# A linear-attention block: buffers for weight sums, and places of a fold's transposes, x statistics and stores in the engines' queues

## The chip, the cores and the metric

The kernel runs on one core of a Trainium2 chip. A core has five engines that each work through a queue of their own in order: TensorE (PE, with its weight loads shown apart as PEld), VectorE (DVE), ScalarE (ACT), GpSimd (POOL) and SyncE (SP), which here only issues DMAs. An instruction waits at the head of its queue until the semaphores it needs have come; what stands behind it on the same engine waits too. The metric is the device time of one launch in microseconds (us). A profiled execution gives the span from the first to the last instruction, and PE's granted clock.

## The reference

All tensors are float32, with S = 2048 rows, D = 1024 columns, 32 heads of 32, and a hidden width of 3584.

```
qkv   = layernorm(x) @ wqkv                       # q, k, v: 32 heads of 32
pq,pk = q_h @ w_phi[h],  k_h @ w_phi[h]           # per head
phi   = concat(softmax(p), softmax(-p))           # for q and for k
o     = phi_q (phi_k^T v) / (phi_q sum(phi_k) + 1e-6)
h     = x + o @ wo
out   = h + relu(layernorm(h) @ w1) @ w2
```

## The kernel before

**Precision.** A float32 product is made of three matmuls: each operand is split into a high part and a low part (high by ACT with a rounding copy, low as the difference, on DVE or POOL), and `mm3` (L180 to L183) adds high x high, high x low and low x high.

**Items and steps.** The work of PE is a list of items. A projection item (`project`, L489) multiplies one tile of 128 rows of x with 8 weight units of 128x512, one unit to a step: so an item has 8 steps of three matmuls. The first half of the rows comes first: items 0 to 31 make k and v (four groups `s` of weights, each over 8 row tiles), items 32 to 47 make q (two groups). Then the second half of the rows, then attention, the output projection, and the two MLP products. The other engines' work is set beside these steps by hand: `do(n, k, f)` puts a call at step k of item n, `when(step, f)` the same with step = 8n + k. The calls are run in the order of the steps when the program is written, so a step sets the order within each engine's queue and not a time: an engine whose queue does not wait can be ahead of PE.

**Weight units.** `Units` (L68 to L136) loads each unit into one of six `raw` tiles (SP, L320 to L334) and splits it into one of ten `w` places: ACT at L124, then POOL or DVE at L128. A load is put into SP's queue as soon as, in program order, a raw tile has been split and the unit is "ready"; it waits there until that split has really been done. Two places are over when a group of 8 units is in use, so the first two splits of the next group come early and the other six follow one by one as PE leaves the old units. A group changes at steps 64, 128, 192, 256 (to q) and 320.

**The fold.** The feature weights `w_phi` are multiplied into the k and q weights on the chip, in eight parts p = 0 to 7. For part p, `wt_load` (L269) loads two tiles `wt`, `fold_part` (L281) makes 32 small matmuls into two `tp` and two `mm` banks and transposes them on DVE, eight instructions of 128x256 (L299), into the tile `wp` (one buffer); `fold_store` (L303) writes it to memory in two halves, and `fold_ready` (L309) lets `Units` load the units made of it. Parts 1 to 3 serve the k groups 1 to 3, parts 4 to 7 the two q groups. The `mm` banks (four) are also those of the items; an item's bank is given back by `kv_first` (DVE, L423 to L427).

**Weight sums.** The MLP uses sums and differences of blocks of w1 and w2. There are 56 of them to be made, number n at step 24 + 10 n (64 later from some point on): `t_load` (L343) loads a tile `b` of 128x4x256 (SP), four `t_sum` (L353, POOL) work in it, and `t_store` (L359, SP) writes it to memory. Their tile has two buffers, in the pool `tsp`.

**x statistics.** For the row tiles 8 to 15 the layer norm's statistics are made early, at steps from 80 + 16 (t - 8): `ln_load` (SP, L214), ten steps on `ln_stats` (DVE, L220 to L222), and three steps on `ln_power` (POOL, L229 to L231). `xin` has two buffers. The row tiles 1 to 7 are normalised and transposed between steps 4 and 52 with a table of their own.

Of the kernel before, what the change touches and what calls it, by code (L numbers as in the profile page):

```python
# [9 lines left out]
F32 = mybir.dt.float32  # L10
# [5 lines left out]
P = 128  # L16
S = 2048
D = 1024
# [5 lines left out]
NK = D // P  # L24
# [115 lines left out]
def kernel(  # L140
# [12 lines left out]
    v, act, pool, pe, sp = nc.vector, nc.scalar, nc.gpsimd, nc.tensor, nc.sync  # L153
# [9 lines left out]
    def mm_bank():  # L163
        return psum.tile([P, 512], F32, name="mm", bufs=4)

    def tp_bank():
        return psum.tile([P, 512], F32, name="tp", bufs=2)
# [20 lines left out]
    def do(n, k, f, *args):  # L188
        at[n, k].append((f, args))
# [17 lines left out]
    xin, xst, xnt = {}, {}, {}  # L207
# [52 lines left out]
    tsp = kps.enter_context(tc.tile_pool(name="tsum", bufs=1, side="right"))  # L260
    folds = ExitStack()
    fp = folds.enter_context(tc.tile_pool(name="fold", bufs=2))
# [3 lines left out]
    wt_of = {}  # L266
    folded = set()

    def wt_load(p, eng, cols=slice(0, D)):  # L269
        for i in range(2):  # L270
            j = 8 + 2 * p + i if p < 4 else 2 * (p - 4) + i
            if (p, i) not in wt_of:
                wt_of[p, i] = fp.tile([P, D], F32, name="wt", bufs=4)
            eng.dma_start(wt_of[p, i][:, cols], wqkT[j][:, cols])

    def fold_mm(p, k, ps, sides=(0, 1)):
# [4 lines left out]
    def fold_part(p):  # L281

        banks = [tp_bank(), tp_bank(), mm_bank(), mm_bank()]
        for i in range(2):
            w = wt_of[p, i].rearrange("e (k c d) -> e k c d", k=NK, c=4)
            for c in range(4):
                for h in range(4):
                    rows = slice(32 * h, 32 * (h + 1))
                    pe.matmul(banks[h][32 * c:32 * (c + 1), 256 * i:256 * (i + 1)], wphi[rows, (2 * p + i) % 8, :],
                              w[rows, :, c, :], start=True, stop=True)  # L290
        wp_of[p] = wp = fp.tile([P, NK, 256], F32, name="wp", bufs=1)
        for h, ps in enumerate(banks):

            if p < 4:
                dst = wp.rearrange("d k (i h f) -> d i h k f", i=2, h=4)[:, :, h]
            else:
                dst = wp.rearrange("d k (r i c f) -> d i c r k f", r=2, i=2, c=2)[:, :, h // 2, h % 2]
            for i in range(2):
                v.transpose(dst[:, i], ps[:, 256 * i:256 * (i + 1)].rearrange("p (k d) -> p k d", k=NK))  # L299

    wp_of = {}
# [38 lines left out]

    tsum = {}

    def t_load(w, p, j):  # L343
        cols = slice(256 * j, 256 * (j + 1))
        b = tsp.tile([P, 4, 256], F32, name="b", bufs=2)
        src = (w1 if w == 1 else w2)[2 * p:2 * p + 2, :, :, cols]
        sp.dma_start(b, src.rearrange("a b p f -> p (a b) f"))
        for r in range(2):
            for c in range(2):
                tsum[j, r, c] = b[:, 2 * c + r if w == 1 else 2 * r + c, :]  # L350
        tsum[j] = b
# [12 lines left out]
    def first_values():  # L364

        for k in range(0, NK, 2):
            if k == 4:
                ln_load(("x", 1), x_part(1))
            place = W.raws.take()
            t = place[1]  # L370
            sp.dma_start(t.rearrange("p (k f) -> p k f", k=2), wv[0, k:k + 2].rearrange("k p f -> p k f"))
            for i in range(2):
                first_raw[k + i] = t[:, 256 * i:256 * (i + 1)], place
        W.loaded = W.done = NK
# [460 lines left out]
    def item(gen, *args, keys):  # L835
        items.append((gen, args + (keys,)))
        steps.extend((k,) for k in keys)
        return len(items) - 1

    kv_n, q_n, wo_n, up_n, down_n = {}, {}, {}, {}, {}  # L840
# [9 lines left out]
    for b, tiles in enumerate(groups):  # L850
        for hf in range(2):

            pairs = b == 0 and hf == 0
            for j in range(0, 4, 2 if pairs else 1):
# [3 lines left out]
                for half in range(2):  # L858
                    n = item(wo_pair, tiles[j:j + 2], hf, half, keys=[("wo", hf, 4 * half + k // 2) for k in range(8)])
# [18 lines left out]
    def x_part(t):  # L878
        return [x[t * P:(t + 1) * P, :]]
# [6 lines left out]
    def when(step, f, *args):  # L886

        if step < 8 * first_up:
            do(step // 8, step % 8, f, *args)
        else:  # L890
            do(first_up + (step - 8 * first_up) // 4, step % 4, f, *args)
# [4 lines left out]
    for t in range(1, NT):  # L896
        n = t - 1 if t < HT else q_n[1, t - HT] + 1
        turn = 8 * n + 1
        if t < HT:
            stages = X_STEPS.get(t, (turn - 22, turn - 12, turn - 9, turn - 6, turn, turn + 3))  # L900
        else:

            early = 80 + 16 * (t - HT)
            when(early, ln_load, ("s", t), x_part(t))
            when(early + 10, ln_stats, ("s", t))
            when(early + 10, xin.pop, ("s", t))
            when(early + 13, ln_power, ("s", t))
            load_ = turn - 88 + 8 * (t - HT) if t < HT + 4 else turn - 36
            stages = (load_, None, None, turn - 8, turn, turn + 3)
        for step, f, *args in zip(stages, (ln_load, ln_stats, ln_power, ln_norm), [("x", t)] * 4):  # L910
            if step is not None:
                when(step, f, *args, *([x_part(t)] if f is ln_load else []))
        do(n, 0, x_open, t)
        for j in range(2):
            when(stages[4 + j], ln_turn, ("x", t), j, lambda t=t: xT[t])


    for i, j in enumerate((2, 3, 0, 1)):
# [1 line left out]
        if i % 2:  # L920
            when(8 * (1 + i // 2) + 2 + 4 * (i % 2) + 3, fold_store, 0, 1 - i // 2)
        when(40, fold_ready, 0, j // 2)
    for p, n in zip(range(1, 8), (3, 6, 10, 14, 18, 22, 26)):
        do(n, 6, fold_part, p)
        for j in range(2):
            when(8 * n + 6 + 5 + j, fold_store, p, j)
            when(8 * n + 6 + 13 + j, fold_ready, p, j)
        if p < 7:
            do(n - 1, 2, wt_load, p + 1, sp)


    for (hf, s, t), n in kv_n.items():
# [106 lines left out]
    def up_step(b, p, m):  # L1039

        return up0 + 4 * (up_n[b, p, m] + 1 - first_up)

    for j, m in enumerate(UP):

        for g in range(2):
            step = up0 + (8 * j + (-62, -32)[g] if j < 4 else 6 * (j - 4) + 10 + 2 * g)
# [4 lines left out]
            step = up_step(0, NP - 1, m) + 3 * j  # L1051
# [13 lines left out]
    for n, (w, p, j) in enumerate((w, p, j) for w in (1, 2) for p in range(NP) for j in range(2)):  # L1065
        step = 24 + 10 * n
        if step > 8 * q_n[1, 0] - 20:
            step += 64
        when(step, t_load, w, p, j)
        for k in range(4):  # L1070
            when(step + 7 + k, t_sum, j, k)
        when(step + 13, t_store, w, p, j)

    for b in range(2):
        for m in DOWN:
            n = down_n[b, m, NP - 1] + 1
            name, more = {1: "x1", 5: "x4", 6: "x2", 4: "x3"}.get(m), \
# [17 lines left out]
    wphi = fp.tile([P, 8, 32], F32, name="wphi", bufs=1)  # L1095
    sp.dma_start(wphi, w_phi.rearrange("(j i) e f -> i e j f", i=4))
    wt_load(0, sp, slice(0, 256))
    ln_load(("x", 0), [x[0:P, 0:512], x[0:P, 512:1024]])
    wt_load(0, sp, slice(256, D))
    first_values()  # L1100
    wt_load(1, sp)
    ident = consts.tile([P, P], F32, name="ident")
    make_identity(nc, ident)
    ones = consts.tile([P, P], F32, name="ones")
# [97 lines left out]
```

## Time and profile before

| what | value |
|---|---|
| time, median of 3 runs | 1923.57 us (1922.38 to 1924.74) |
| time of the profiled execution | 1924.54 us |
| span of the profiled execution | 1922.8 us |
| mean granted PE clock | 0.996 |
| POOL, DVE, ACT busy | 967.0, 1044.2, 741.9 us |
| DMA | 432.17 MB, 224 GB/s over the span |

A row of a timeline gives the start, the duration, the engine, the line and what it writes and reads; in brackets stands how long the engine stood idle before it and what it waited for. A row of the waits gives the engine, the line, whom it waited for, the total in us, how often, and the longest. A row of windows gives the stretch, its length, the busy time of PE, PEld, DVE, ACT and POOL, the granted clock, the DMA engines' share and GB/s. PE's rows are pipelined, so consecutive ones overlap.

### The profile page before, as it was taken

The numbers are of one execution on the slowest core, as the hardware profiler recorded it, in microseconds if no ns is written. First come the engines' busy times: TensorE is split into PE (matmuls) and PEld (weight loads), VectorE is DVE, ScalarE is ACT, GpSimd is POOL, SyncE is SP. The second block draws the span as 40 slices with busy tenths as digits, with TensorE's granted clock in tenths as the row PEclk, the third lists the DMA queues.
The fourth block names the chain that finished last, engine by engine and source line by source line (L and its number), as shares of the span: only waits on it lengthen the run. The fifth ranks groups of instructions, "written<-read, shape, count | busy, mean of one in ns | idle before, by whom it ended". The sixth has DMA issues, their size and how long they took to land.

```text
span 1922.8 us, 31955 instructions
## 1 busy us (share of the span) xinstructions
PE 1894.4 (99%) x11640; PEld 1539.5 (80%) x11640; DVE 1044.2 (54%) x1752; ACT 741.9 (39%) x1318; POOL 967.0 (50%) x935
## 2 busy tenths in 40 slices
PE   8989999999999999999999999999999999999999
PEld 7767778887877777788888888888888888888887
DVE  6867668776779866546554465333533333333333
ACT  5322225322223211245544464444444444444442
POOL 3677752789955988423333222222244444444443
PEclk9999999999999999999999999999999999999999
DMA  6877786666566657787777796656677677767775
GB/s 216 271 252 257 225 262 197 214 210 199 183 225 200 197 190 255 231 261 237 246 255 249 250 298 213 197 182 193 202 246 234 192 237 224 252 211 220 214 217 177
DMA packets 292733, 432.17 MB, mean 225 GB/s; under 512 B 24160, under 2 KB 150368, under 8 KB 292576
## 3 DMA queue, kind: packets, MB, share of 16 engines
q1 hardware_dynamic: 275680, 413.36, 67.8%
q10 hardware_dynamic: 16896, 16.78, 2.6%
q8 instruction: 91, 1.49, 0.3%
q14 instruction: 66, 0.54, 0.1%
HBM read 292.68 MB, written 137.36 MB: 224 GB/s over the span
## 4 chain that ended last, share of the span: by engine, by line
PE 83%; POOL 7%; DMA 4%; issue 2%; DVE 2%; ACT 0%; SPq 0%; POOLq 0%; DVEq 0%; ACTq 0%
PE mm L181 21%; PE mm L182 20%; PE mm L183 20%; POOL b L357 4%; PE ac L181 4%; PE ac L182 4%; PE ac L183 4%; PE tp L182 2%; PE tp L183 2%; PE tp L181 2%; POOL w L128 2%; DMA b<-in_w_dram 1%; PE tp L244 1%; DMA t<-b 1%; DMA xin<-in_x_dram 1%
## 5 line engine op out<-in xcount | busy, mean ns | idle before, releaser
L128 POOL TENSOR_TENSOR w<-raw,w 128x512 fp32r<-128x512 f32 x355 | 472.0, 1331 | 718.7 <-ACT w L124 678.0
L124 ACT ACTIVATE w<-raw 128x512 fp32r<-128x512 f32 x686 | 409.0, 626 | 516.6 <-PE mm L183 253.2
L128 DVE TENSOR_TENSOR w<-raw,w 128x512 fp32r<-128x512 f32 x331 | 269.0, 813 | 529.3 <-ACT w L124 528.6
L181 PE MATMUL mm<-w,xT 128*128 128x512 f32 x768 | 311.1, 405 | 5.0 <-DVE ke L427 5.0
L182 PE MATMUL mm<-w,xT 128*128 128x512 f32 x768 | 303.7, 395 | 12.5 <-POOL w L128 12.3
L183 PE MATMUL mm<-w,xT 128*128 128x512 f32 x768 | 301.7, 393 | 0.0
L181 PE MATMUL mm<-hT,w 128*128 128x512 f32 x672 | 262.6, 391 | 0.0
L183 PE MATMUL mm<-hT,w 128*128 128x512 f32 x672 | 261.6, 389 | 0.0
L182 PE MATMUL mm<-hT,w 128*128 128x512 f32 x672 | 261.5, 389 | 0.0
L357 POOL TENSOR_TENSOR b<-b 128x256 f32<-128x256 f32 x224 | 181.7, 811 | 108.8 <-DMA b<-in_w_dram 98.0
L182 PEld LDWEIGHTS mm<-w,xT 128*128 128x128 f32 x768 | 145.8, 190 | 47.0 <-POOL w L128 17.2
L181 PEld LDWEIGHTS mm<-w,xT 128*128 128x128 f32 x768 | 145.7, 190 | 42.5 <-issue 11.7
L183 PEld LDWEIGHTS mm<-w,xT 128*128 128x128 f32 x768 | 145.5, 190 | 30.9
L181 PE MATMUL mm<-w 128*128 128x512 f32 x392 | 152.5, 389 | 0.0
L182 PE MATMUL mm<-w 128*128 128x512 f32 x392 | 152.5, 389 | 0.0
L183 PE MATMUL mm<-w 128*128 128x512 f32 x392 | 152.5, 389 | 0.0
L183 PEld LDWEIGHTS mm<-hT,w 128*128 128x128 f32 x672 | 126.1, 188 | 26.5
L182 PEld LDWEIGHTS mm<-hT,w 128*128 128x128 f32 x672 | 126.2, 188 | 25.7
L181 PEld LDWEIGHTS mm<-hT,w 128*128 128x128 f32 x672 | 126.2, 188 | 25.7
L431 ACT ACTIVATE ke<-ke 128x512 f32<-128x512 f32 x64 | 40.4, 631 | 156.5 <-DVE ke L427 156.4
L183 PEld LDWEIGHTS mm<-w 128*128 128x128 f32 x392 | 73.6, 188 | 15.3
L181 PEld LDWEIGHTS mm<-w 128*128 128x128 f32 x392 | 73.6, 188 | 15.3
(165 smaller groups left out, 3141.7 us busy)
## 6 DMA issues: line engine op xcount, KB each, us to landing
raw<-t SPq DMA_DIRECT2D x224, 256.0 KB, 3.8
raw<-ad SPq DMA_DIRECT2D x196, 256.0 KB, 3.0
raw<-in_w_dram SPq DMA_DIRECT2D x168, 256.0 KB, 3.0
b<-in_w_dram SPq DMA_DIRECT2D x56, 512.0 KB, 4.1
t<-b SPq DMA_DIRECT2D x56, 512.0 KB, 4.5
ad<-c SPq DMA_DIRECT2D x112, 256.0 KB, 3.6
ad<-s SPq DMA_DIRECT2D x84, 256.0 KB, 3.9
ed<-qe ACTq DMA_DIRECT2D x32, 512.0 KB, 4.4
```

Of the source, the lines that this page charges most:

```text
L124: nc.scalar.activation(w[:, 0, :], raw[1], AF.Copy)
L128: eng.tensor_tensor(out=w[:, 1, :], in0=raw[1], in1=w[:, 0, :].bitcast(F32), op=ALU.subtract)
L181: pe.matmul(ps, a_hi, b_hi, start=first, stop=False, skip_group_check=more)
L182: pe.matmul(ps, a_hi, b_lo, start=False, stop=False, skip_group_check=more)
L183: pe.matmul(ps, a_lo, b_hi, start=False, stop=last, skip_group_check=more)
L244: pe.transpose(pt[:, k, :], xn[:, (4 * j + k) * P:(4 * j + k + 1) * P], ident)
L357: pool.tensor_tensor(out=tsum[j, *out], in0=tsum[j, *a], in1=tsum[j, *b], op=ALU.subtract)
L431: act.activation(e_of[key], e_of[key], AF.Exp)
```

## The change

Four things are moved, and no operation is added or left out.

- The `wt` tiles get two buffers instead of four. Part p is loaded at the beginning of item n - 2, where n is the item of its fold (part 1 at item 1 instead of in the prologue).
- The parts 2 to 7 are folded at items 8, 12, 16, 20, 24 and 28 instead of 6, 10, 14, 18, 22 and 26, part 1 one step later in item 3. `fold_part` makes only the transposes of the two `mm` banks (heads 2 and 3); those of the `tp` banks (heads 0 and 1) come four steps later, for part 1 at once. Stores come 14 and 16 steps after the fold's step instead of 5 and 6, readiness 24 and 26 steps after it instead of 13 and 14.
- The tile `b` gets two more buffers, in the fold's pool `fp`, for n with n mod 4 of 2 or 3, as long as step + 20 is before item 32, which holds for n up to 21. For all n up to 21 the sums come 12 steps behind the load instead of 7, and the store 19 instead of 13.
- The early statistics of x tiles 8 to 15 come 14 steps behind their load instead of 10, `ln_power` 17 instead of 13.

```diff
-                wt_of[p, i] = fp.tile([P, D], F32, name="wt", bufs=4)
+                wt_of[p, i] = fp.tile([P, D], F32, name="wt", bufs=2)
...
-        wp_of[p] = wp = fp.tile([P, NK, 256], F32, name="wp", bufs=1)
-        for h, ps in enumerate(banks):
-
+        wp_of[p] = fp.tile([P, NK, 256], F32, name="wp", bufs=1)
+        fold_banks[p] = banks
+        fold_turn(p, (2, 3))
+        if p == 1:
+            fold_turn(p, (0, 1))
+
+    fold_banks = {}
+
+    def fold_turn(p, heads):
+
+        wp = wp_of[p]
+        for h in heads:
+            ps = fold_banks[p][h]
             if p < 4:
...
-    def t_load(w, p, j):
+    def t_load(w, p, j, place):
         cols = slice(256 * j, 256 * (j + 1))
-        b = tsp.tile([P, 4, 256], F32, name="b", bufs=2)
+        b = place.tile([P, 4, 256], F32, name="b", bufs=2)
...
-            when(early + 10, ln_stats, ("s", t))
-            when(early + 10, xin.pop, ("s", t))
-            when(early + 13, ln_power, ("s", t))
+            when(early + 14, ln_stats, ("s", t))
+            when(early + 14, xin.pop, ("s", t))
+            when(early + 17, ln_power, ("s", t))
...
-    for p, n in zip(range(1, 8), (3, 6, 10, 14, 18, 22, 26)):
-        do(n, 6, fold_part, p)
+    for p, n in zip(range(1, 8), (3, 8, 12, 16, 20, 24, 28)):
+        do(n, 6 if p > 1 else 7, fold_part, p)
+        if p > 1:
+            when(8 * n + 10, fold_turn, p, (0, 1))
         for j in range(2):
-            when(8 * n + 6 + 5 + j, fold_store, p, j)
-            when(8 * n + 6 + 13 + j, fold_ready, p, j)
-        if p < 7:
-            do(n - 1, 2, wt_load, p + 1, sp)
+            when(8 * n + 6 + 14 + 2 * j, fold_store, p, j)
+            when(8 * n + 6 + 24 + 2 * j, fold_ready, p, j)
+        do(max(n - 2, 1), 0, wt_load, p, sp)
...
-        when(step, t_load, w, p, j)
+        far = step + 20 < 8 * q_n[0, 0]
+        when(step, t_load, w, p, j, fp if far and n % 4 > 1 else tsp)
         for k in range(4):
-            when(step + 7 + k, t_sum, j, k)
-        when(step + 13, t_store, w, p, j)
+            when(step + (12 if far else 7) + k, t_sum, j, k)
+        when(step + (19 if far else 13), t_store, w, p, j)
...
-    wt_load(1, sp)
```

## The prediction

> **What bounds the kernel now.** I read the page first, then the waits by engine for the first 310 us, then a table of windows over the same stretch, and last the timelines around each place where PE stands. A step below is one `k` of one item, as in the code: eight steps to an item, three matmuls to a step.
>
> ```profile
> PE 1894.4 (99%) x11640; PEld 1539.5 (80%) x11640; DVE 1044.2 (54%) x1752; ACT 741.9 (39%) x1318; POOL 967.0 (50%) x935
> 120.00:140.00 20.00, 14.94 (x102) 11.21 (x101) 14.46 (x33) 5.75 (x11) 13.57 (x14) 0.91 0.71 227
> 140.00:180.00 40.00, 37.64 (x344) 28.99 (x343) 25.45 (x60) 5.75 (x12) 26.04 (x36) 0.96 0.86 291
> 240.00:260.00 20.00, 16.03 (x89) 11.62 (x88) 8.79 (x14) 3.88 (x5) 16.28 (x17) 0.91 0.81 250
> 260.00:400.00 140.00, 140.00 (x764) 115.03 (x763) 108.64 (x186) 55.80 (x83) 70.91 (x75) 1.00 0.69 224
> ```
>
> PE is the bound: only standing PE time can be won, since the change takes no matmul away. In the windows' rows (length, then PE, PEld, DVE, ACT, POOL, granted clock, DMA share, GB/s) PE has holes between 120 and 260 us and none from 260 to 400. The granted clock, too, is below 1.00 in the holed stretches. These are PE's own rows after each hole, with the idle time in brackets:
>
> ```profile
> 126.70 0.39 PE L183 MATMUL mm<-w,xT 128*128 128x512 f32 x1
> 126.92 0.39 PE L181 MATMUL mm<-w,xT 128*128 128x512 f32 x1
> 132.12 0.79 PE L182 MATMUL mm<-w,xT 128*128 128x512 f32 x1 [4.81 <-POOL w L128]
> 132.71 0.63 PE L183 MATMUL mm<-w,xT 128*128 128x512 f32 x1
> 133.14 0.63 PE L181 MATMUL mm<-w,xT 128*128 128x512 f32 x1
> 135.29 0.55 PE L182 MATMUL mm<-w,xT 128*128 128x512 f32 x1 [0.25 <-POOL w L128]
> 152.47 0.75 PE L181 MATMUL mm<-w,xT 128*128 128x512 f32 x1 [2.36 <-DVE ke L427]
> 189.43 0.50 PE L182 MATMUL mm<-w,xT 128*128 128x512 f32 x1 [1.14 <-POOL w L128]
> 208.49 0.47 PE L181 MATMUL mm<-w,xT 128*128 128x512 f32 x1 [2.62 <-DVE ke L427]
> 242.76 0.50 PE L182 MATMUL mm<-w,xT 128*128 128x512 f32 x1 [1.50 <-POOL w L128]
> 245.94 0.49 PE L182 MATMUL mm<-w,xT 128*128 128x512 f32 x1 [1.51 <-POOL w L128]
> 247.85 0.63 PE L182 MATMUL mm<-w,xT 128*128 128x512 f32 x1 [0.96 <-POOL w L128]
> ```
>
> Matmuls start 126.92 - 126.70 = 0.22 us apart though one takes 0.39 (they are pipelined), so a step is about 0.67 us. The first two rows are the last before the first hole. After it they start 133.14 - 132.71 = 0.43 apart: half speed. I name the holes by their time: **A** at 132, **B** at 152, **C** at 189, **D** at 208, **E** at 243 to 248. A, C and E wait for a split of a weight on POOL (L128); B and D wait for DVE to give back a matmul bank (L427).
>
> What makes POOL and DVE late (the waits of the first 310 us: who waited at which line for whom, us in total, how often, the longest; then rows of timelines):
>
> ```profile
> POOL b L357 <- DMA b<-in_w_dram: 63.4, 16, 10.4
> DVE st L220 <- DMA xin<-in_x_dram: 29.6, 8, 8.1
> SPq L347 <- DMA t<-b: 69.0, 18, 7.6
> SPq L324 <- POOL w L128: 27.5, 9, 8.7
> 115.27 0.53 SPq L360 DMA_DIRECT2D t<-b  x1
> 122.89 0.38 SPq L347 DMA_DIRECT2D b<-in_w_dram  x1
> 127.32 0.72 POOL L357 TENSOR_TENSOR b<-b 128x256 f32<-128x256 f32 x1 [3.91 <-DMA b<-in_w_dram]
> 140.37 0.62 SPq L214 DMA_DIRECT2D xin<-in_x_dram  x1
> 146.69 1.29 DVE L220 BATCH_NORM_STATS2 st<-xin 128x6 f32<-128x512 f32 x2 [8.05 <-DMA xin<-in_x_dram]
> 175.28 1.57 POOL L357 TENSOR_TENSOR b<-b 128x256 f32<-128x256 f32 x2 [3.08 <-DMA b<-in_w_dram]
> 187.67 3.40 POOL L128 TENSOR_TENSOR w<-raw,w 128x512 fp32r<-128x512 f32 x2
> 193.42 3.46 SPq L324 DMA_DIRECT2D raw<-wpq  x2
> 202.47 1.29 DVE L220 BATCH_NORM_STATS2 st<-xin 128x6 f32<-128x512 f32 x2 [7.37 <-DMA xin<-in_x_dram]
> 227.51 2.37 POOL L357 TENSOR_TENSOR b<-b 128x256 f32<-128x256 f32 x3 [3.71 <-DMA b<-in_w_dram]
> 246.54 1.25 POOL L128 TENSOR_TENSOR w<-raw,w 128x512 fp32r<-128x512 f32 x1
> ```
>
> It is one ring. SP holds the load of `b` number n until the store of number n-2 has landed (two buffers; 69.0 us of SP's time, 18 times). POOL then stands at the sum, and behind the sum in POOL's queue stands the split that PE needs. **A**: the store went out at 115.27, the next load only at 122.89, POOL stood 3.91 us until 127.32, and only then come the sum, other work and the split; PE resumes at 132.12. **C** and **E**: POOL stands 3.08 us at 175.28 and 3.71 us at 227.51 and then works without a break into the group change; E's last split ends at 246.54 + 1.25 = 247.79, and PE resumes at 247.85. **B** and **D**: SP waits for the same late splits to free raw tiles (3.46 us at 193.42), so the load of x goes out late (140.37, and after 193.42 + 3.46 = 196.9), DVE stands 8.05 and 7.37 us at its statistics, and the bank eviction behind them is late for PE.
>
> **What the change does to these, term by term.** The number of matmuls, sums, transposes, splits and DMAs stays the same; only buffers and places in the queues move.
>
> *The holes' size.* Idle time is 4.81 + 0.25 + 2.36 + 1.14 + 2.62 + 1.50 + 1.51 + 0.96 = 15.15. The bracket starts when the last matmul has ended, 0.39 - 0.22 = 0.17 after the next one could have started: seven times 0.17 adds 1.2. Clock: 0.09 x 20 + 0.04 x 40 + 0.09 x 20 = 5.2 us lost at half speed in three places. Together **21.5 us**.
>
> Here a rule can be weighed. The trace shows half speed behind a 2.36 us hole (133 and 152 alike) and behind E's three holes, none above 1.51. The Trainium skill, page "TensorE: Matmul & The Clock Gate", section "Why this matters for your kernels", says that gaps under about 3 us keep the full clock. By it only A would cost clock, and the sum would be 18.1; the trace disagrees in B and E, and I keep 21.5.
>
> *Four buffers until the fold pool closes* (loads 0 to 21, ending at step 234). A load now waits for the store four numbers back, which is in order 21 steps before it instead of 7: 14 us against some 5. The page's landing times are these:
>
> ```profile
> b<-in_w_dram SPq DMA_DIRECT2D x56, 512.0 KB, 4.1
> t<-b SPq DMA_DIRECT2D x56, 512.0 KB, 4.5
> L357 POOL TENSOR_TENSOR b<-b 128x256 f32<-128x256 f32 x224 | 181.7, 811 | 108.8 <-DMA b<-in_w_dram 98.0
> ```
>
> A turn of a buffer is load 4.1 + four sums 3.2 (at 811 ns) + store 4.5, about 12 us. Two buffers allow one unit per 6 us, just under the 10 steps (6.7 us) that are asked; every delay stays in the ring. Four allow one per 3. With sums 12 steps (8 us) behind their load, POOL need not stand. So A goes, and C and E lose the 3 to 4 us by which POOL entered late. The store's six steps more keep SP from waiting on POOL in front of its x loads.
>
> *x statistics four steps later*: 14 steps are 9.4 us. B's x load was 146.69 - 140.37 = 6.3 us under way, D's 202.47 - 196.9 = 5.6. Issued in time they land before DVE asks; with splits no longer late SP does issue them in time. B and D go. The wait that is added is only `ln_power` on POOL, moved along by the same four steps; its consumer is the normalisation far later.
>
> *Fold later and halved.* All 7 x 8 transposes stay. In order the folds of steps 54, 86, 118, 150, 182 and 214 become 70, 102, 134, 166, 198 and 230, away from the group changes at 64, 128 and 192. The second half of the transposes lands in the gap that DVE spends on the exponent. I put no separate gain on it; below zero it could cost what it took beside a split, some 1 us for C. The two `wt` buffers: a load is now 22 steps (14.7 us) ahead of its fold's matmuls, and the buffers it takes were read 10 steps before it or earlier; the matmuls of the item beside it hide it, and PE stands if it lands later than that. I take 0.
>
> *What is late next.* (1) Item 8. Weights of the second group are loaded at step 54 instead of 43, for use at 64. SP runs ahead of PE, so the step is not the time:
>
> ```profile
> 51.70 0.22 POOL L229 TENSOR_SCALAR sc<-mv 128x1 f32<-128x1 f32 x1 [2.94 <-DVE mv L222]
> 53.52 0.42 SPq L320 DMA_DIRECT2D raw<-wpk  x1
> 74.06 0.40 PE L181 MATMUL mm<-w,xT 128*128 128x512 f32 x1
> raw<-wpk SPq DMA_DIRECT2D x56, 128.0 KB, 3.6
> L128 POOL TENSOR_TENSOR w<-raw,w 128x512 fp32r<-128x512 f32 x355 | 472.0, 1331 | 718.7 <-ACT w L124 678.0
> ```
>
> Loads went out at 53.52 for a first use at 74.06. In the new order the first sums stand behind x tile 6's power (51.70 on POOL) instead of ahead of it, the store of `b` 0 behind them, and the fold's stores and the next `b` store behind that. I estimate the raw loads at about 63: 51.7 + two rounds of sums and a zacc. The first split is ready at about 63 + 3.6 (landing) + ACT's part and POOL's, 1.3 at most each, = 69.2, under 74; but POOL then owes eight sums' rest, splits and zaccs by step 70, and the last splits come within 1 us of their use. Bounds 0 to 5 us (3 us late plus a half-speed stretch); I take **1.5**. (2) Steps 186 to 189: sums 15 now fall between the splits of the group change at 192: four sums are 3.2 us, of which some 1 us stays: **1.0**, bounds 0 to 3. (3) Step 244: load 22 has only its own pair of buffers again and follows the store of 20 by one step, not seven; POOL no longer brings along the 3.71 us that it stood at 227.51, so I take **0.5**, bounds 0 to 5. (4) Unseen rest, small waits at new places: **1.0**, bounds -1 (the prologue no longer shares its transfers with the `wt` pair that now loads at step 8) to 3.
>
> Contention between POOL and DVE is in the rows: the two splits at 187.67 took 1.70 each against 1.33 on average. The same operations overlap as before, so no term.
>
> Sum: 21.5 - 1.5 - 1.0 - 0.5 - 1.0 = **17.5 us**. The profiled execution took 1924.5 (span 1922.8 and what lies around it), 1 us above the median 1923.6; taken from the execution it gives 1907.0, from the median **1906.1**, which I predict.
>
> **The rivals.**
> *Partial.* A, B and D go, C and E stay, because POOL is short of time at a group change whatever it had before: C cost 1.14 + 0.17 = 1.3, E 3.97 + 3 x 0.17 + 1.7 of clock = 6.2, together 7.5 of the 21.5. With the new terms (1) and (3) at mid range, 2.5 each, the gain is 21.5 - 7.5 - 5 = 9: **1914.6**. For it: E's last split ends a long run of POOL work. Against it: the 3.71 us it stood just before.
> *SP stays the bound.* The raw ring, not `b`, holds SP: 27.5 us of waiting on POOL's splits (L324) remain in the code. Then x loads stay late and so do sums, and what A gives is taken at item 8: **1922**. Against it: the splits were late through `b`, as A shows.
> *Slower.* One mechanism, at item 8: SP's queue now has the fold's stores behind the store of `b` 0 and the raw loads behind the store of `b` 1. It decides from raw loads later than about 74.1 - 6.2 = 68 us; each us beyond is a us of PE, and half clock on top. If sums wait for DVE there as the row at 51.70 does, and SP stays as tight further on, holes of A's kind come back and 5 us are added: **1929**.
>
> The skill's rule of the clock, if it held for the new trace, would only lower the gain: 18.1 - 4 = 14, so 1909.5, inside the forecast's own range; it is no case by itself.
>
> **How the numbers follow.** Forecast (gain 13 to 22, 1901.5 to 1910.5) 0.57; partial (gain 4 to 13) 0.25; SP stays the bound 0.11; slower 0.07. A measurement here tells 0.2%, 3.8 us, from no change. Faster is forecast and partial, 0.82; same 0.11; slower 0.07. The range takes the forecast's upper bound with a little for terms at zero, 1900, and most of the partial case, 1918.
>
> **What would show it.** Right: in the first 310 us POOL's wait at L357 for `b` falls from 63.4 to under 15; SP's wait at L347 for `t<-b` from 69.0 to under 30; DVE's wait at L220 for x from 29.6 to under 15; no PE hole over 2 us between 100 and 230; granted clock 1.00 there; items start evenly from item 16 on. Wrong: a hole before item 9 (term 1), around step 256 (term 3), or bank waits on L427 that stay while POOL's waits are gone, which would take B and D out of my ring.

## The result and the profile after

| kernel | median us | range, runs | ratio to before, 95% interval |
|---|---|---|---|
| before | 1923.31 | 1922.38 to 1924.74, 4 | |
| changed | 1910.54 | 1908.41 to 1912.33, 4 | 0.9933 (0.9915 to 0.9950) |

The change makes the kernel 12.8 us faster, 0.67%; 17.5 had been forecast (1906.1, range 1900 to 1918). The profiled execution took 1910.06 us with a span of 1908.3. From here on, A to E are the five holes of the kernel before, at 132, 152, 189, 208 and 243 to 248 us.

Windows of the changed kernel (start and end, length, then busy PE, PEld, DVE, ACT and POOL, the granted clock, DMA share, GB/s):

```profile
70.00:90.00 20.00, 15.85 (x161) 10.95 (x160) 16.05 (x31) 7.41 (x14) 18.41 (x18) 0.91 0.53 161
120.00:140.00 20.00, 20.00 (x200) 15.43 (x201) 18.03 (x33) 6.46 (x13) 19.18 (x22) 1.00 1.02 342
140.00:180.00 40.00, 40.00 (x351) 32.32 (x344) 33.12 (x71) 10.81 (x21) 31.28 (x38) 1.00 0.98 323
220.00:240.00 20.00, 19.29 (x157) 15.20 (x156) 11.19 (x23) 7.60 (x13) 16.98 (x16) 1.00 0.74 249
```

From 120 to 180 us PE has no hole any more and runs at full clock. Of E a small one is left (0.71 us at 232). A new place stands at 70 to 90 us: 20 - 15.85 = 4.15 us without work, and clock 0.91. The waits of the first 310 us, to be read against those of before:

```profile
PE mm L182 <- POOL w L128: 4.9, 4, 3.1
POOL b L367 <- DMA b<-in_w_dram: 43.4, 11, 16.9
DVE st L220 <- DMA xin<-in_x_dram: 1.7, 1, 1.7
SPq L357 <- DMA t<-b: 25.4, 5, 7.9
SPq L334 <- POOL w L128: 15.8, 7, 5.3
```

DVE's wait for x fell from 29.6 to 1.7 us, SP's for the stores of `b` from 69.0 to 25.4, SP's for splits of q's raw tiles (L324 before, L334 now) from 27.5 to 15.8. POOL's wait for `b` fell only from 63.4 to 43.4, yet the holes behind it are gone: POOL's idle time away from a change of group cost PE nothing here.

The new place, in the changed kernel's timelines of SP, ACT, POOL and PE:

```profile
59.16 2.25 SPq L274 DMA_DIRECT2D wt<-in_wqkT_dram  x2
62.90 0.59 SPq L330 DMA_DIRECT2D raw<-wpk  x1
63.54 0.47 SPq L331 DMA_DIRECT2D raw<-in_wv_dram  x1
70.49 1.38 ACT L124 ACTIVATE w<-raw 128x512 fp32r<-128x512 f32 x2 [6.38 <-DMA raw<-in_wv_dram]
71.20 1.28 POOL L128 TENSOR_TENSOR w<-raw,w 128x512 fp32r<-128x512 f32 x1 [8.25 <-ACT w L124]
71.80 0.40 PE L181 MATMUL mm<-w,xT 128*128 128x512 f32 x1
77.21 1.17 POOL L367 TENSOR_TENSOR b<-b 128x256 f32<-128x256 f32 x1
78.34 1.25 POOL L128 TENSOR_TENSOR w<-raw,w 128x512 fp32r<-128x512 f32 x1
79.65 0.80 PE L182 MATMUL mm<-w,xT 128*128 128x512 f32 x1 [3.08 <-POOL w L128]
85.47 0.39 PE L181 MATMUL mm<-w,xT 128*128 128x512 f32 x1
```

This is term (1) of the prediction, the second group of weights at item 8. The raw loads went out at 62.90, where the prediction had put them (63). But the second half of that tile, issued at 63.54, let ACT start only at 70.49, 6.9 us later, against the 3.6 it was given. POOL, 8.25 us without work, then had splits and the sums of number 2 to make at once, in turn: the sum at 77.21 stands ahead of the split at 78.34, and PE resumes at 79.65, when that split is done. Item 8 lasts 85.47 - 71.80 = 13.7 us.

### The profile page after: what moved, and what is told of

It reads as the page before. It is cut to its first block, busy times and chain, and to the rows that moved or that the text cites. A ratio compares the mean times of both kernels' runs of the same rounds, so it can differ in the third digit from the quotient of the medians.

```text
span 1908.3 us, 31967 instructions
## 1 busy us (share of the span) xinstructions
PE 1889.7 (99%) x11640; PEld 1539.3 (81%) x11640; DVE 1048.7 (55%) x1752; ACT 741.6 (39%) x1318; POOL 969.1 (51%) x935
## 4 chain that ended last, share of the span: by engine, by line
PE 86%; POOL 6%; DMA 4%; issue 1%; DVE 1%; ACT 1%; SPq 0%; POOLq 0%; DVEq 0%; ACTq 0%
PE mm L181 22%; PE mm L182 21%; PE mm L183 21%; PE ac L181 4%; PE ac L182 4%; PE ac L183 4%; POOL b L367 3%; PE tp L182 2%; PE tp L181 2%; PE tp L183 2%; POOL w L128 2%; DMA b<-in_w_dram 2%; PE tp L631 1%; DMA t<-b 1%; PE tp L244 1%
## 5 line engine op out<-in xcount | busy, mean ns | idle before, releaser
L181 PEld LDWEIGHTS mm<-w 128*128 128x128 f32 x392 | 73.6, 188 | 15.2
L183 PEld LDWEIGHTS mm<-w 128*128 128x128 f32 x392 | 73.6, 188 | 15.2
L182 PEld LDWEIGHTS mm<-w 128*128 128x128 f32 x392 | 73.6, 188 | 15.2
```

The costliest lines, as they stand in the source:

```text
L181: pe.matmul(ps, a_hi, b_hi, start=first, stop=False, skip_group_check=more)
L182: pe.matmul(ps, a_hi, b_lo, start=False, stop=False, skip_group_check=more)
L183: pe.matmul(ps, a_lo, b_hi, start=False, stop=last, skip_group_check=more)
```

## The experiments

Each line is an edit of the changed kernel or of the one before, timed against the kernel before on the same chip.

| run | median us | ratio to before, 95% interval |
|---|---|---|
| two_buffers | 1919.42 | 0.9979 (0.9969 to 0.9989) |
| x_stats_back | 1910.84 | 0.9933 (0.9918 to 0.9948) |
| ready_early | 1902.75 | 0.9892 (0.9878 to 0.9907) |
| wt_late | 1907.25 | 0.9914 (0.9898 to 0.9931) |
| fold_alone | 1918.72 | 0.9975 (0.9963 to 0.9987) |
| buffers_alone | 1918.57 | 0.9969 (0.9956 to 0.9981) |
| sums_old_places | 1907.03 | 0.9914 (0.9899 to 0.9929) |
| early_and_q | 1902.51 | 0.9890 (0.9875 to 0.9905) |
| ready_late | 1909.28 | 0.9922 (0.9907 to 0.9937) |
| fold_ready_soon | 1919.96 | 0.9980 (0.9968 to 0.9991) |
| early_and_22 | 1901.86 | 0.9883 (0.9867 to 0.9900) |
| ready_late_buffers | 1909.57 | 0.9923 (0.9904 to 0.9942) |

**two_buffers**: the changed kernel with the old buffers, sums and stores of `b`.

```diff
-        far = step + 20 < 8 * q_n[0, 0]
+        far = False
```

> The changed kernel with b in its two old buffers, sums 7 and stores 13 steps behind the load; the fold's new places and the later x statistics stay. If the ring of two b buffers made the holes A to E, holes of that kind come back: over 10 us of PE idle time between 100 and 250 us, POOL's wait for b in the first 310 us back to 55 or more (changed kernel 43.4, before 63.4), SP's wait for t<-b to 60 or more (25.4), and a time of 1917 to 1925. If the fold's places and the later statistics took the holes away (rival), PE stays free of holes from 100 to 250 and the time is within 3 us of 1910.5. The hole at item 8 (76 us) should shrink, since the first sums stand ahead of x tile 6's power again, and the fold's stores of part 1 go out earlier.

Waits in the first 310 us, and PE's rows behind its largest holes between 120 and 250 us:

```profile
POOL b L367 <- DMA b<-in_w_dram: 70.0, 17, 19.0
SPq L357 <- DMA t<-b: 84.2, 23, 8.4
128.19 0.50 PE L182 MATMUL mm<-w,xT 128*128 128x512 f32 x1 [3.81 <-POOL w L128]
133.44 0.79 PE L182 MATMUL mm<-w,xT 128*128 128x512 f32 x1 [3.37 <-POOL w L128]
140.00:220.00 80.00, 80.00 (x714) 63.65 (x713) 60.84 (x141) 18.66 (x36) 58.62 (x72) 1.00 0.82 274
```

8.9 us of the gain are lost, and hole A is back, in two pieces, and E after 234 us. But from 140 to 220 PE has no hole: B, C and D stay away with the ring of two in full force (84.2 us of SP's waiting). They have another cause. E's return (4.1 us of idle time) shows that E does need the four buffers in the changed kernel.

**x_stats_back**: the statistics at their old steps.

```diff
-            when(early + 14, ln_stats, ("s", t))
+            when(early + 10, ln_stats, ("s", t))
...
-            when(early + 17, ln_power, ("s", t))
+            when(early + 13, ln_power, ("s", t))
```

> The changed kernel with the x statistics 10 and 13 steps behind their load again. If SP's lateness through the ring was the cause of holes B and D, x lands in time without the four steps: at most 2 us more than 1910.5, DVE's wait at L220 for x under 8 us in all. If the four steps themselves took B and D away (rival), DVE stands at L220 for 15 us or more and holes that wait for the bank eviction return, 4 to 7 us: 1914.5 to 1917.5.

1910.84 beside the changed kernel's 1910.54, and DVE's wait for x is 4.3 us instead of 1.7. The later statistics did nothing that can be measured here.

**ready_early**: part 1 alone gets its old stores and readiness.

```diff
-            when(8 * n + 6 + 14 + 2 * j, fold_store, p, j)
-            when(8 * n + 6 + 24 + 2 * j, fold_ready, p, j)
+            when(8 * n + 6 + (14 + 2 * j if p > 1 else 5 + j), fold_store, p, j)
+            when(8 * n + 6 + (24 + 2 * j if p > 1 else 13 + j), fold_ready, p, j)
```

> The changed kernel with part 1's stores 5 and 6 steps and its readiness 13 and 14 steps behind its fold, as before; so SP issues the raw loads of the second group ahead of the first b stores. If the hole at item 8 comes from those loads going out late (62.9 us instead of 53.5), all of it goes: PE has no wait for a split between 70 and 85 us, clock 1.00 there, 6 to 8 us less, 1902.5 to 1904.5. If POOL's crowding (sums 2 between the splits) makes the hole (rival), half or more stays: 1907 or more.

SP's and PE's timelines and the window:

```profile
56.21 0.62 SPq L330 DMA_DIRECT2D raw<-wpk  x1
72.01 0.40 PE L181 MATMUL mm<-w,xT 128*128 128x512 f32 x1
79.70 0.47 PE L181 MATMUL mm<-w,xT 128*128 128x512 f32 x1
70.00:90.00 20.00, 19.85 (x216) 14.69 (x215) 13.34 (x33) 4.05 (x8) 17.29 (x19) 1.00 0.72 229
```

The raw loads go out at 56.21 instead of 62.90, and the hole is gone: item 8 takes 79.70 - 72.01 = 7.7 us, 6.0 less than the 13.7 of the changed kernel. The time is 1902.75, 7.8 us under the changed kernel's and 1.1% under the kernel before. Sums 2 still stand between the splits, so POOL's crowding alone does not make the hole; whether late loads alone would, sums_old_places shows below.

**wt_late**: part 2's `wt` pair behind the raw loads.

```diff
-        do(max(n - 2, 1), 0, wt_load, p, sp)
+        do(*((7, 4) if p == 2 else (max(n - 2, 1), 0)), wt_load, p, sp)
```

> The changed kernel with the wt pair of part 2 loaded at step 60, behind the raw loads of the second group instead of ahead of them; the raw loads go out at the same place otherwise. If the burst of transfers just ahead of the raw loads (1 MB of wt, and stores and b) makes them land in 7 us instead of 3.6, the splits of item 8 come some 3 to 4 us earlier and the hole shrinks by 3 to 6 us: 1905 to 1907.5. If the order in SP's queue alone counts (rival), SP reaches the raw loads only 2 us earlier and the time is 1908 to 1909.

The median, 1907.25, lies in the range for the burst, but the profile does not bear that out: its span is 1907.4 us against 1908.3, and PE still stands there once for 3.1 us. With the `wt` pair behind them the raw loads still take 5.8 us from the issue of their second half (63.52) to ACT's start (69.29), so by this profile some 1 us of the 6.9 is that pair. What makes up the rest is not shown.

**fold_alone**: only the fold's places and the two `wt` buffers are new (the edits of two_buffers and x_stats_back together).

> The changed kernel with both b (two buffers, sums 7 and stores 13 behind the load) and the x statistics (10 and 13) as before; only the fold's places and the two wt buffers are new. Two buffers alone brought back holes A and E but not B, C and D; statistics alone brought back nothing. If B and D need the ring and the early statistics together, they come back here beside A and E: DVE's wait at L220 for x 15 us or more, holes behind the bank eviction, 1921 to 1927. If the fold's new places took B, C and D away (rival), the time stays within 3 us of the run with two buffers: 1917 to 1922, with DVE's wait under 8 us.

```profile
SPq L357 <- DMA t<-b: 79.4, 21, 7.1
SPq L334 <- POOL w L128: 7.6, 3, 5.2
DVE st L220 <- DMA xin<-in_x_dram: 8.7, 5, 4.8
132.81 0.79 PE L182 MATMUL mm<-w,xT 128*128 128x512 f32 x1 [5.09 <-POOL w L128]
140.00:220.00 80.00, 80.00 (x714) 63.63 (x713) 62.12 (x143) 18.65 (x36) 63.01 (x76) 1.00 0.83 279
```

Hole A is there in full (5.09 us and one of 2.19 before it), and B, C and D are gone with neither the buffers nor the statistics. SP's wait for splits at q's raw tiles is 7.6 us against 27.5 before. So it is something in the fold's part of the change. The profile is of the fastest of six runs (1914.77 us; median 1918.72).

**buffers_alone**: the kernel before with four buffers and no later sums.

```diff
+        far = step + 20 < 8 * q_n[0, 0]
-        when(step, t_load, w, p, j)
+        when(step, t_load, w, p, j, fp if far and n % 4 > 1 else tsp)
...
-                wt_of[p, i] = fp.tile([P, D], F32, name="wt", bufs=4)
+                wt_of[p, i] = fp.tile([P, D], F32, name="wt", bufs=2)
...
-            do(n - 1, 2, wt_load, p + 1, sp)
+        do(max(n - 2, 1), 0, wt_load, p, sp)
```

> The kernel before with four buffers for b up to number 21 (sums still 7 and stores 13 steps behind the load), which needs two wt buffers loaded two items ahead of each fold; the fold's places and the x statistics stay as before. If the ring of two buffers made A and E and fed B and D, POOL's wait for b in the first 310 us falls to 45 or less, A and E shrink to under 2 us each, and the time is 1903 to 1912, without a hole at item 8 since part 1 keeps its early stores. If the sums' later places were needed (rival), POOL still stands at the sums between 100 and 250 us and half or more of the holes stay: 1914 to 1920.

```profile
SPq L347 <- DMA t<-b: 14.4, 4, 6.2
SPq L324 <- POOL w L128: 31.3, 9, 9.8
POOL b L357 <- DMA b<-in_w_dram: 74.3, 18, 16.4
DVE st L220 <- DMA xin<-in_x_dram: 20.1, 5, 7.9
147.99 0.47 PE L181 MATMUL mm<-w,xT 128*128 128x512 f32 x1 [1.46 <-DVE ke L427]
234.94 0.79 PE L182 MATMUL mm<-w,xT 128*128 128x512 f32 x1 [1.95 <-POOL w L128]
```

The ring of two is gone (69.0 to 14.4 us), and yet POOL waits longer for `b` (74.3) than before (63.4), DVE still stands 20.1 us at x, and the time is 1918.57, in the rival's range. SP still waits in q's raw loads (31.3 against 27.5). A shrinks to 3.3 us of idle time, C and most of D go, B keeps 1.5 behind the bank eviction and E 3.6. So the ring that the prediction described held part of the holes at most. Two further waits of PE, 0.5 and 0.6 us, are for `wt`, which here has two buffers with the folds at their old places.

**sums_old_places**: the changed kernel with sums 7 and stores 13 steps behind the load, in four buffers.

```diff
-            when(step + (12 if far else 7) + k, t_sum, j, k)
-        when(step + (19 if far else 13), t_store, w, p, j)
+            when(step + 7 + k, t_sum, j, k)
+        when(step + 13, t_store, w, p, j)
```

> The changed kernel, four buffers, with sums 7 and stores 13 steps behind the load. If the later places only serve to cover the load's landing, POOL's wait for b grows by 5 to 15 us but the four buffers keep PE's holes A to E away between 100 and 250; and since the first sums stand ahead of x tile 6's power again, the hole at item 8 shrinks to under 2 us: 1903 to 1907. If the later places are what removed A and E (rival), holes of 3 us or more come back there: 1908 to 1916.

SP, POOL and the window at item 8:

```profile
62.08 0.46 SPq L330 DMA_DIRECT2D raw<-wpk  x1
73.65 3.45 POOL L128 TENSOR_TENSOR w<-raw,w 128x512 fp32r<-128x512 f32 x2
77.06 3.96 POOL L367 TENSOR_TENSOR b<-b 128x256 f32<-128x256 f32 x4
70.00:90.00 20.00, 19.73 (x212) 14.05 (x211) 18.66 (x38) 6.79 (x14) 18.10 (x18) 1.00 0.64 184
```

Two holes of 1.0 and 1.1 us stay at A, none at half clock, and item 8 has nearly none (0.18 us). Yet the raw loads go out at 62.08, only 0.8 us ahead of the changed kernel's, and ACT starts on them at 68.74. What is different is POOL: four splits come first, and the sums stand behind them, from 77.06. wt_late, where ACT starts little later, at 69.29, but sums stand between the splits, keeps its 3.1 us. So late loads alone do not make the hole at item 8 either: it takes late loads and sums between the splits, and ready_early and this run each take one of the two away. 1907.03 is under the changed kernel's 1910.54: the later sums are worth some 2 us at A, and they cost more at item 8.

This run is also one edit away from two_buffers: only the two more buffers. They take the time from 1919.42 to 1907.03, and A from 7.2 us of idle time to 2.1, and E from 4.1 to 0.7.

**early_and_q**: ready_early, with sums and stores of 20 and 21 at their old places.

```diff
-            when(step + (12 if far else 7) + k, t_sum, j, k)
-        when(step + (19 if far else 13), t_store, w, p, j)
+            when(step + (12 if far and n < 20 else 7) + k, t_sum, j, k)
+        when(step + (19 if far and n < 20 else 13), t_store, w, p, j)
```

> The changed kernel with part 1's stores and readiness as before, and besides with sums 20 and 21 at 7 and their stores at 13 steps, so that load 22 follows the store of 20 by seven steps and not one and sums 21 stand ahead of the splits for q. If load 22 and the crowded sums make the last hole (1.1 us at step 256), it goes and the time is 1901 to 1902; if POOL's work at that change of group is too much in any order (rival), the hole stays or grows: 1902.5 to 1905.

No difference: 1902.51, and the same hole of 0.7 us. Load 22 is not what makes it.

**ready_late**: the kernel before with one edit, the step at which parts 2 to 7 are called ready.

```diff
-            when(8 * n + 6 + 13 + j, fold_ready, p, j)
+            when(32 * p + 30 + 2 * j if p > 1 else 8 * n + 6 + 13 + j, fold_ready, p, j)
```

> The kernel before with one edit: for parts 2 to 7 only the readiness comes at the changed kernel's steps (94, 126, 158, 190, 222, 254); transposes, stores, buffers and statistics stay. If B and D come from SP being held by raw loads of the next group that stand ahead of the x loads in its queue, this edit alone removes them: no hole behind the bank eviction (L427) between 140 and 215 us, SP's wait at L324 on POOL's splits from 27.5 to under 12, DVE's wait at L220 for x from 29.6 to under 15, A and E stay, and the time is 1915 to 1919. If it was the transposes beside the group changes (rival), B and D stay: 1921 to 1926.

Waits, PE from 140 to 220 us, and the two holes left at A:

```profile
SPq L347 <- DMA t<-b: 70.5, 22, 7.6
SPq L324 <- POOL w L128: 10.2, 6, 5.2
DVE st L220 <- DMA xin<-in_x_dram: 4.9, 4, 2.0
127.66 0.50 PE L182 MATMUL mm<-w,xT 128*128 128x512 f32 x1 [2.36 <-POOL w L128]
130.39 0.79 PE L182 MATMUL mm<-w,xT 128*128 128x512 f32 x1 [0.88 <-POOL w L128]
140.00:220.00 80.00, 80.00 (x683) 63.32 (x682) 58.71 (x133) 18.12 (x35) 61.98 (x75) 1.00 0.79 257
```

1909.28, well under the 1915 to 1919 expected: this edit alone gives as much time as the whole change. With two buffers (70.5 us of waiting for stores, as before), early statistics and the folds beside the group changes, B, C and D are gone, and E, which was expected to stay, is down to 0.7 us. The queue of SP shows why for B. First the kernel before:

```profile
123.95 2.12 SPq L320 DMA_DIRECT2D raw<-wpk  x1
132.09 0.33 SPq L320 DMA_DIRECT2D raw<-wpk  x1
136.64 0.51 SPq L347 DMA_DIRECT2D b<-in_w_dram  x1
```

And the same stretch with late readiness:

```profile
124.09 0.37 SPq L347 DMA_DIRECT2D b<-in_w_dram  x1
124.56 1.16 SPq L320 DMA_DIRECT2D raw<-wpk  x1
130.26 0.62 SPq L214 DMA_DIRECT2D xin<-in_x_dram  x1
```

The raw loads of the *next* group are put into SP's queue as soon as a split is called; they then wait there for that split to be done, at PE's pace. Before, load 10 of `b` and the load of x stood behind them and went out at 136.64 and 140.37; with the units called ready later the load of `b` is ahead of them, at 124.09, and x goes out at 130.26. Nothing needs the next group's raw tiles so soon.

Readiness is not the whole of the fold's part, though. fold_alone has the same late readiness for these parts and two buffers too, and is 9 us slower (1918.72), with 7.3 us of idle time at A against 3.2 here. Which of its other places costs that (transposes, stores, `wt` or part 1) no run shows.

**fold_ready_soon**: fold_alone with stores and readiness at their old distances.

```diff
-            when(8 * n + 6 + 14 + 2 * j, fold_store, p, j)
-            when(8 * n + 6 + 24 + 2 * j, fold_ready, p, j)
+            when(8 * n + 6 + 5 + j, fold_store, p, j)
+            when(8 * n + 6 + 13 + j, fold_ready, p, j)
```

> The fold-alone kernel (b and statistics as before) with the stores 5 and 6 and the readiness 13 and 14 steps behind each fold, as before; the transposes keep their new places and halves. If the late readiness removed B and D, holes behind the bank eviction come back and SP's wait at L324 rises to 20 us or more: 1921 to 1926. If the transposes' places did it (rival), they stay away: 1916 to 1920.

Mixed. SP's wait at L334 rises to 22.8 us as expected and PE's work from 140 to 220 us falls to 75.5 of 80, but the holes are at 178 to 183 (waits for splits) and at 210 (0.9 us, for `wt`), and none is behind L427; the time, 1919.96, is not apart from fold_alone's 1918.72. It shows that readiness, with the stores ahead of it, sets SP's wait, and that this wait alone does not set the time. It is no full test of B and D: since the folds stand later, part 2 is ready at step 83, sooner than the changed kernel's 94 but still 16 steps later than the 67 of the kernel before. What the transposes' places do beside it stays open.

**early_and_22**: ready_early, with sums and store of number 22 behind the splits for q.

```diff
-            when(step + (12 if far else 7) + k, t_sum, j, k)
-        when(step + (19 if far else 13), t_store, w, p, j)
+            when(step + (12 if far or n == 22 else 7) + k, t_sum, j, k)
+        when(step + (19 if far or n == 22 else 13), t_store, w, p, j)
```

> The changed kernel with part 1's stores and readiness as before, and besides sums and store of number 22 at 12 and 19 steps, behind the splits for q instead of between them. If POOL's order at that change of group makes the last hole (1.1 us), it goes and the time is 1901 to 1902.2; if the six splits, four of them on POOL, are themselves too much there (rival), the hole stays within 0.3 us: 1902.3 to 1903.5.

1901.86, the lowest median of all, 1.2% under the kernel before, though its runs overlap with those of ready_early and early_and_q. No wait of PE for a split is left in the first 310 us: the last hole was POOL's order, sums between splits.

**ready_late_buffers**: buffers_alone with ready_late's edit.

> The kernel before with two edits: the late readiness of parts 2 to 7, and four buffers for b up to number 21 (with the two wt buffers that need it); sums, stores, transposes and x statistics stay at their old steps. If readiness takes B to E and the four buffers take what is left of A (7 us with its half clock in the run with late readiness alone), the time is 1902 to 1905 and POOL's wait for b falls below 50 us. If the later sums are needed for A (rival: with four buffers and the old sums it kept two holes of 1.4 us), A keeps 2 to 4 us: 1905 to 1908.

Neither: 1909.57, no faster than ready_late alone. In its profile, of the slowest of four runs, A keeps one hole of 1.8 us, but E is back with three, and POOL waits 65.2 us for `b`. Why E is back is not shown: ready_late has sums 20 to 22 and the q splits in the same order on POOL, and only 0.7 us there. So the four buffers, worth 12 us in the changed kernel with the same old sums (sums_old_places beside two_buffers), are worth nothing here.

## Why the prediction was right in sign and size, and where its reasons failed

- **The holes are what could be won: right.** All of the gain lies before 280 us, and no work of PE changed. Of the 21.5 us that A to E were put at, 0.7 is left, item 8 costs 6.0 and a new stretch at half clock at 523 us costs 1.7: 13.1 us remain, beside 12.8 measured between the medians and 14.5 between the two profiles' spans. The 12.8 lies just under the forecast case's own bounds (13 to 22) and at the top of the partial case's; but C and E, which were to stay in that case, did not.
- **A belongs to the two buffers: right.** It has 3 to 7 us of idle time and a stretch at half clock in every run with two buffers, 2 to 3 us and full clock with four and the old sums, and is gone with four and the later sums.
- **B and D "go" through the ring and the later x statistics: the step that failed.** The chain from late x loads to the bank eviction was read rightly; its head was not. What held SP were the raw loads of the next group, and the fold's later readiness, on which the prediction put "no separate gain", took that away: in the kernel before, this alone is enough (ready_late); in the changed one no run parts it cleanly from the fold's other new places. C went with it. E is mixed: ready_late takes it to 0.7 us with two buffers, but two_buffers, as late in readiness, has it back, so in the changed kernel it also hangs on the four buffers, as predicted. B, C and D with their clock are about 8 of the 21.5 us; that they came off although their cause was misread is luck. The statistics, which the prediction named for B and D, did nothing measurable. The rival "SP stays the bound" had the right queue (27.5 us at L324 in the profile) but concluded that nothing would help; the prediction's answer, that the splits were late through `b`, held for A and in part for E.
- **Item 8, term (1): right in place and mechanism, wrong in size.** It named late raw loads and the sums that POOL then still owes, and both are needed (ready_early, sums_old_places). It was taken at 1.5 with bounds of 0 to 5; ready_early measures 6.0 in item 8. The issue time was right to 0.1 us; the landing was taken at the median of 3.6 us and was 6.9. This is the largest miss of the sum: without the hole the time is 1902.75 (ready_early).
- **Terms (2) and (3)**: nothing at 186 to 189 (1.0 taken); 0.7 us at step 256 and its start-up (0.5 taken). The cause of the latter was not load 22 (early_and_q) but sums 22 between the splits (early_and_22).
- **Signs**: SP's and DVE's waits and the clock came as forecast; POOL's wait for `b`, forecast under 15 us, was 43.4. That sign was badly chosen, since POOL's waits elsewhere cost nothing here. Of the signs of being wrong, a hole before item 9 and one around step 256 both came.
- **Clock.** The changed kernel has two stretches at half speed: at 80 us behind holes of 0.34, 0.73 and 3.08 us, and at 523. The second in the changed kernel, and then the same hole in the kernel before:

```profile
522.29 0.50 PE L182 MATMUL mm<-w,xT 128*128 128x512 f32 x1 [1.40 <-POOL w L128]
520.00:530.00 10.00, 8.60 (x59) 6.37 (x59) 4.03 (x6) 1.06 (x1) 9.29 (x9) 0.83 0.52 158
538.40 0.50 PE L182 MATMUL mm<-w,xT 128*128 128x512 f32 x1 [1.40 <-POOL w L128]
530.00:540.00 10.00, 8.42 (x76) 6.32 (x65) 4.60 (x8) 2.06 (x4) 10.00 (x10) 1.00 0.70 226
```

In the changed kernel a hole of 1.40 us costs another 0.17 x 10 = 1.7 us; in the kernel before, a hole as long left the clock at 1.00, and so did D's 2.62 us (1.00 from 200 to 220 us). So the length of one hole did not decide it, and a clock term read from one trace need not come again in the next. The Trainium skill, page "TensorE: Matmul & The Clock Gate", section "Why this matters for your kernels", would let gaps under about 3 us pass; half speed behind 1.40 us here, as behind B and E before, does not agree.

## What to carry to other kernels

A load that waits in an in-order DMA queue for its buffer blocks every load behind it, as the raw loads at 123.95 us held the load of `b` until 136.64: do not let it into the queue earlier than its use needs, even if its source is long ready. "Who waits longest" names a queue, not a cause: to find what holds it, look at what stands at its head and whether that is needed yet, and undo one part at a time. When work is set later to clear one place, follow its stores to the next group's loads, and do not size their landing by a median over the whole kernel (here 3.6 us against 6.9). And test a cause from both sides: the hole at item 8 needed two things at once, and each run that took one away looked like the proof of that one.

## What the runs showed that was not expected

One line about when units may be loaded was worth as much (14 to 15 us) as the whole change. And the gains do not add: four buffers are worth 12 us in the changed kernel with the old sums, and nothing beside late readiness in the kernel before (1909.57 against 1909.28).
